# Hash attention and a squared-ReLU feed-forward block: the last pair of the last chunk in wide form, gates moved to ScalarE, second-layer sums by quarters

## The chip, the cores and the metric

The kernel runs on one core of a Trainium2 chip. The metric is the device time of one execution in microseconds. The profile is that of one execution on the same kind of core; its times are counted from its first instruction. The engines are TensorE (PE; PEld is its weight load), VectorE (DVE), ScalarE (ACT), GpSimd (POOL) and SyncE (SP). A "q" behind an engine's name marks its sequencer, which issues DMAs.

## The reference

Attention over hash buckets, and then a feed-forward block on its output:

```python
q_bucket, k_bucket = ...            # six sign bits of q @ proj and of k @ proj
scores = np.where(q_bucket == k_bucket, scale * q @ k.T, -1e9)
attn = softmax(scores);  x = (attn @ v) as (3072, 512)
h = x @ w_in                        # (3072, 2048)
r = np.maximum(h, 0.0);  g = r * r
out = g @ w_out                     # (3072, 512)
```

All values are fp32. The shapes are 4 batches, 8 heads, 768 tokens and 64 dimensions for the attention, and 3072 tokens, 512 inputs and 2048 hidden features for the block. The change touches the block alone.

## The kernel before, in words

**Stages.** Attention comes first, two heads at a time; beside it the weights of the block are read, rounded and stored to DRAM in the forms that the block needs (`round_weight`, `keep_weight`, L185 to L210; the pieces of w_out pass through two buffers named `out_piece`, and L210 stores them). Then come three chunks of 1024 tokens (`i` = 0, 1, 2). Each chunk has a first layer (hidden = x w_in and its gate, the squared ReLU) and a second layer (`project`, out = hidden w_out).

**Products with fewer multiplications.** A product of two 2x2 block matrices is made with seven block products in place of eight (Winograd's form of Strassen's method). The price is sums and differences of blocks before and after. `product` (L972) is the order of these seven: it holds three PSUM accumulators (acc0, acc1, acc2, two buffers each), and `keep` copies partial sums from them to SBUF tiles `one`, `two`, `five` and `three` on ScalarE. Block product 0 opens acc0; 1 goes to acc1; 4, 5 and 2 are added to acc0 one after the other, each after the last partial sum was copied; 3 and 6 go to acc2.

**First layer.** A chunk's 1024 tokens and 2048 hidden features are cut in half, so that a unit of 128 features of the upper and 128 of the lower half needs seven products of 128x128 weights with 512 tokens, each over two blocks of inputs. The results are b11, b12, b21 and b22, each of 8 rows of 128x512. Chunk 0 uses this form alone (`hidden`, L1091). Chunks 1 and 2 work in pairs of units (`n` = 0 to 3, each of two halves) and apply the method a second time inside some of the seven products. A product so treated is seven matmuls of 256 columns for both halves of the pair, in place of four matmuls of 512 columns. `hidden_pair` (L1410) treats three products (A, B, C) so and keeps four as they are; `hidden_wide` (L1314) treats five (A, B, C, D, E) and keeps two. Before the change pairs 0 to 2 of a chunk are wide and pair 3 is `hidden_pair`, in both chunks (L1750). `inner_steps` (L1210) gives the steps of a treated product: its accumulators are acc banks or two side banks (`last0`, `last1`), its intermediate copies go by ScalarE (L1237, L1248, L1251, L1255, L1264) and its adds by VectorE (`add_in`, L1273). Before the change a copy of one partial sum goes into a spare quarter (`spots`) of the tiles of sums.

**Gates.** A gate is either one VectorE instruction that multiplies max(h, 0) with h (`gated`, L1075), or two ScalarE activations in place, Relu and Square (`gate_in`, L1275).

**Order around a pair.** The program's order is the order of each engine's queue; it is written out by hand. `hidden_wide` leaves the end of its work (gates, differences for the second layer) in lists; `behind(m)` runs list m of the pair before at a chosen place of the pair that follows. `hidden_pair` calls `behind` too and leaves nothing. After the first half of pair 3, five `leaf` tiles (w_out parts) are loaded by DMAs that ScalarE issues (`load_leaf`, L1493). `mark` (L1040) squares a piece of q and k on ScalarE with an accumulated maximum, to guard the attention's range; it does not depend on the block.

**Second layer.** `project` (L1568) makes seven products `k` = 0 to 6, each again of seven leaves. `OUTER` (L1475) names the operand of each: b11, b12, b_t, b22, b21, b11, b_t. VectorE makes the sums of these operands as it goes: `inner_sums(k)` makes the two tiles t1, t2 of product k, and the `hook` after its second leaf subtracts t2 from one quarter. Behind product 0 b11 becomes b22 - b_t, and behind product 2 b_t becomes b21 - b11, in two instructions of 2048 elements a partition each (L1693, L1699).

**Memory.** Tiles come from pools that are opened on memory that earlier pools gave back; a tile that lies where an earlier tile was waits for the last users of that one. Pool `p_r` (L953) opens after attention with `one`, NH = 5 tiles `h` (L962, L1083), `two`, `five` and `three`, of 2048 bytes a partition each, in this order, from byte 98,976 on; it lies where the weight stage had its last pieces. `p_k` and `p_y` follow it.

Of the kernel before, what the change touches and what calls it, by code (L numbers as in the profile page):

```python
# [34 lines left out]
def kernel(  # L35
# [686 lines left out]
    def load_unit(n, pool=p_i):  # L722

        if n < NCHUNK * NR and n not in w_unit:
# [13 lines left out]
            if n >= 2 * NR:  # L738
                nc.sync.dma_start(out=five_six(w), in_=w_in_49[pair, :, 3 + half])
# [4 lines left out]
    def sum_unit(n):  # L744


        if NR <= n < 2 * NR and n % NR < NR - 2:
# [6 lines left out]
            nc.gpsimd.dma_start(out=w_in_49[pair, :, 3 + half], in_=five_six(w))  # L754
# [15 lines left out]
    with tc.manual_schedule():  # L770
# [191 lines left out]
        HN, QN, NH = NCH // 2, NCH // 4, 5  # L962
# [9 lines left out]
        def product(n, w, at, bt, c11, c12, c21, c22, hook=None, last=False, beside=None, cuts=1):  # L972
# [16 lines left out]
            def keep(of, name):  # L989
                t = p_r.tile([P, 512], FP32, name=name, bufs=KEPT[name])[:, 0:w]  # L990
                nc.scalar.copy(out=t, in_=acc[of])  # L991
                return t
# [121 lines left out]
        w_inner, t_inner, spots, snaps, now, behind_pair = {}, {}, {}, {}, {}, {}  # L1114
# [77 lines left out]
        def sums_inner(i, js):  # L1192

            for j in js:
                y11, y12, y21, y22 = quarters_x(i, j)
                if j < 3:
                    tile = p_y.tile([P, NQ, QN], FP32, name=f"t{j}", **({"bufs": 2} if j < 2 else {}))
                    t = [tile[:, m] for m in range(NQ - 1)] + [y12]
                    spots[i, j] = tile[:, NQ - 1]
                else:  # L1200
# [3 lines left out]
                t_inner[i, j] = t  # L1204
# [5 lines left out]
        def inner_steps(i, j, side, w):  # L1210

            t1, t2, t4, t3 = t_inner[i, j]
            y11, _, y21, y22 = quarters_x(i, j)
            if i not in snaps:
                snaps[i] = [side_bank(m)[:, 0:QN] for m in range(2)]
            one = three = spots[i, side]
            hs = {}
# [7 lines left out]
            def mul(out, a, b, start, stop):  # L1227
                nc.tensor.matmul(  # L1228
                    out=out, lhsT=w(a), rhs=b, start=start, stop=stop, skip_group_check=True
                )  # L1230

            def step_0():
                a0, a1 = (
                    ps_m.tile([P, 512], FP32, name=f"acc{m}")[:, 0:QN] for m in (0 if j == 4 else 1, 2)
                )
# [5 lines left out]
                hs["a0"] = a0  # L1241

            def step_1():
                last = hs["last"] = (
                    ps_m.tile([P, 512], FP32, name="acc2")[:, 0:QN] if j == 4 else snaps[i][side]
                )
                mul(hs["a0"], 4, t2, False, False)
                nc.scalar.copy(out=hs[0][:, QN:HN], in_=hs["a0"])  # L1248
                mul(last, 3, t1, True, False)
                hs[1] = new(1)  # L1250
                nc.scalar.copy(out=hs[1][:, QN:HN], in_=last)  # L1251

            def step_2():
                mul(hs["a0"], 5, t3, False, False)
                nc.scalar.copy(out=three, in_=hs["a0"])  # L1255
                mul(hs["last"], 6, y22, False, True)

            def adds():
                for unit, by in (0, hs["last"]), (1, three):
                    add_in(hs[unit][:, QN:HN], by)  # L1260

            def step_3():
                mul(hs["a0"], 2, t4, False, True)
                nc.scalar.copy(out=hs[1][:, 0:QN], in_=hs["a0"])  # L1264

            def put(unit, out, other):
                add_in(hs[unit], other)
                gated(out, hs[unit])

            return step_0, step_1, step_2, step_3, put, adds, hs  # L1270
# [43 lines left out]
        def hidden_wide(i, n, half):  # L1314

            r0, r = n, NQ + n
            w, acc, add, keep = outer_steps(i, n, half)
            own = own_factors(w, half)
            if half == 0:
                load_inner(i, n + 1)  # L1320
                load_third_inner(i, n + 1, nc.sync)
                now["A"] = inner_steps(i, 0, 0, w_inner[i, n][0])
                if n == 0:
                    sums_inner(i, (3,))
                now["D"] = inner_steps(i, 3, 1, lambda a: own[a])
            A, D = now["A"], now["D"]
            u0 = D[6]
            add(acc, 0, "11", True, False)
            one = keep(acc, "one")
            if half == 0:  # L1330
# [5 lines left out]
                behind(0)  # L1336
            else:
                B, C = inner_steps(i, 2, 0, w_inner[i, n][2]), inner_steps(i, 1, 1, w_inner[i, n][1])
                E = inner_steps(i, 4, 2, lambda a: own[a])
                B[0]()  # L1340
                C[0]()
                E[0]()
                A[4](1, b11[:, r], one)
                behind(2)
                sum_unit(i * NR + 2 * n + 2)
            add(acc, 4, "t2", False, True)
            two = keep(acc, "two")
            if half == 0:
                A[1]()
                D[1]()  # L1350
                A[2]()
                D[2]()
                A[3]()
                D[3]()
                if n == 0:
                    mark()
                A[5]()
                D[5]()
                add_in(u0[0], two)
                A[4](0, b11[:, r0], one)  # L1360
                sum_unit(i * NR + 2 * n + 1)
                behind(1)
                now["two"] = two
                return
            two_0 = now["two"]
            B[1]()
            C[1]()
            add_in(u0[1], two)
            B[2]()
            C[2]()  # L1370
            B[5]()
            E[1]()
            C[5]()
            B[3]()
            E[2]()
            B[4](0, b12[:, r0], u0[0])
            C[3]()
            E[3]()
            E[5]()
            B[4](1, b12[:, r], u0[1])  # L1380
            hC, hE = C[6], E[6]
            add_to(b22[:, r0], u0[0], hE[0])
            add_to(b22[:, r], u0[1], hE[1])
            add_in(two_0, hE[0])
            add_to(b21[:, r0], hC[0], two_0)
            behind(3)

            def step_0():
                gate_in(b22[:, r0])
                add_in(two, hE[1])  # L1390
                add_to(b21[:, r], hC[1], two)
                for m in r0, r:
                    minus(b_t[:, m], b12[:, m], b11[:, m])
                inner_sums(0, slice(n, n + 1))
                minus(b12[:, r0], b22[:, r0], b12[:, r0])

            def step_1():
                gate_in(b22[:, r])

            def step_2():  # L1400
                gate_in(b21[:, r0])
                minus(b12[:, r], b22[:, r], b12[:, r])

            def step_3():
                gate_in(b21[:, r])

            for m, step in enumerate((step_0, step_1, step_2, step_3)):
                behind_pair[m].append(step)

        def hidden_pair(i, n, half):  # L1410
# [3 lines left out]
            if half == 0:  # L1414
                now["A"], now["C"], now["B"] = (
                    inner_steps(i, j, (0, 0, 1)[j], w_inner[i, n][j]) for j in range(3)
                )
# [6 lines left out]
            else:  # L1424
                B[2]()
                B[5]()
                C[0]()
                A[4](1, b11[:, r], one)
                B[4](0, b12[:, r0], now["two"])
                behind(3)  # L1430
# [14 lines left out]
            if half == 0:  # L1445
                A[2]()
                A[5]()
                B[0]()
                A[4](0, b11[:, r], one)
                add_in(two, five)  # L1450
            else:
                C[2]()
                C[5]()
                add_in(two, five)
                B[4](1, b12[:, r], two)
                minus(b_t[:, r], b12[:, r], b11[:, r])
                inner_sums(0, slice(n, n + 1))
                C[4](0, b21[:, r0], now["three"])
# [8 lines left out]
            else:  # L1467
# [3 lines left out]
                C[4](1, b21[:, r], three)  # L1471
# [95 lines left out]

        def project(i):  # L1568
# [60 lines left out]
            for k in range(7):  # L1629
# [23 lines left out]

                def hook():
                    y21 = b[:, NQ:NR, 0:QN]
                    minus(y21, y21, t2)
                    if marks(i, k):
# [20 lines left out]
                use = uses[k]  # L1678
                product(
                    NQ, QN, a_with_load, bt, lambda *p: use(0, *p), lambda *p: use(1, *p),  # L1680
                    lambda p: use(2, p, None), lambda *p: use(3, *p), hook,
                    (i, k) == (NCHUNK - 1, 6), mark if marks(i, k) else None,
                )
# [302 lines left out]
```

## Time and profile before

| what | value |
|---|---|
| time, median of 3 runs | 850.16 us (849.66 to 850.66) |
| profiled execution: its own time | 851.49 us |
| its span, first to last instruction | 849.9 us |
| granted TensorE clock, mean | 0.999 |
| first layer of chunk 0 starts | 314.06 us |
| first layer of chunk 1 | 494.98 to 584.77 us |
| first layer of chunk 2 | 669.66 to 758.46 us |
| last second layer starts | 758.46 us |

A line of a timeline has the start, the duration, the engine, the line of the kernel, the operation, the tile written and the tiles read, their shapes and the number of instructions merged; square brackets hold the idle time of the engine before it and what ended it. A matmul in fp32 has two records, of half its time each; the duration of a record is longer than the distance to the next because matmuls overlap, so distances of starts are the measure of TensorE's pace. A line of a group has the busy time, the mean of one in ns, and the idle time before them. A line of a stretch has the busy time and count of each engine, the granted clock, the share of the DMA engines and GB/s.

### The profile page before, as it was taken

What the parts mean: (1) busy time and instruction counts of PE and PEld (TensorE: products, weight loads), DVE (VectorE), ACT (ScalarE), POOL (GpSimd) and SP (SyncE); (2) the same over time, 40 slices, a digit from 0 to 9 for tenths busy, and PEclk for the clock granted to TensorE, in tenths of its full rate; (3) what the DMA queues carried; (4) which work ended last, traced back from release to release, by engine and by line L of the source; (5) the groups of instructions that cost most, each with busy time, mean ns of one, the idle gap of its engine ahead of it and who ended that gap; (6) DMA issues with size and microseconds to landing.
All of it is one profiled execution on the core that took longest, in us unless ns stands there. A gap on an engine that the chain in (4) does not pass through costs nothing.

```text
span 849.9 us, 17478 instructions
## 1 busy us (share of the span) xinstructions
PE 841.6 (99%) x6698; PEld 555.4 (65%) x6698; DVE 758.5 (89%) x1087; ACT 439.8 (52%) x833; POOL 171.0 (20%) x289
## 2 busy tenths in 40 slices
PE   9999999999999999999999999999999999999997
PEld 4444444444475445544788877767888777768885
DVE  4898999999999988989899989988988988888876
ACT  5887777878777762222211146775232457753210
POOL 1321121303221201643121220001211300021103
PEclk9999999999999999999999999999999999999999
DMA  9966999989996426999977994418878964157666
GB/s 185 201 130 138 185 186 201 207 173 224 249 245 202 158 69 245 330 312 306 359 254 220 275 226 145 146 50 292 298 214 244 247 207 145 51 169 213 201 166 128
DMA packets 237304, 174.10 MB, mean 205 GB/s; under 512 B 165224, under 2 KB 195248, under 8 KB 237216
## 3 DMA queue, kind: packets, MB, share of 16 engines
q1 hardware_dynamic: 196976, 90.14, 43.3%
q0 software_dynamic: 16992, 44.02, 16.5%
q10 hardware_dynamic: 23248, 38.78, 14.7%
q8 instruction: 54, 0.88, 0.5%
q14 instruction: 34, 0.28, 0.1%
HBM read 129.51 MB, written 42.73 MB: 203 GB/s over the span
## 4 chain that ended last, share of the span: by engine, by line
PE 95%; DMA 2%; DVE 1%; ACTq 0%; issue 0%; ACT 0%; POOL 0%; SPq 0%; POOLq 0%; DVEq 0%
PE acc L984 40%; PE st L478 18%; PE xo L532 14%; PE acc L1228 10%; PE acc L1298 8%; PE last L1228 3%; PE tot L589 1%; PE hash L396 1%; DMA bits<-signed 1%; DMA out_dram<-h 1%; PE tp L342 0%; DMA qk_nat<-in_q_dram 0%; ACTq L1499 0%; DVE h L1522 0%; DVE o L1288 0%
## 5 line engine op out<-in xcount | busy, mean ns | idle before, releaser
L484 ACT ACTIVATE e<-st 128x768 f32<-128x768 f32 x192 | 155.5, 810 | 56.8 <-PE st L478 52.5
L532 PE MATMUL xo<-e,v_nat 64*64 64x385 f32 (+1 forms) x1520 | 156.7, 483 | 0.0
L984 PE MATMUL acc<-b,leaf 128*128 128x256 f32 x600 | 133.1, 379 | 0.0
L984 PEld LDWEIGHTS acc<-b,leaf 128*128 128x128 f32 x600 | 113.9, 190 | 16.1 <-issue 0.5
L478 PE MATMUL st<-feat 64*64 64x384 f32 x1056 | 109.3, 483 | 0.0
L444 POOL DMA_DIRECT2D bits<-signed x120 | 62.1, 522 | 196.5 <-ACT signed L433 194.7
L532 PEld LDWEIGHTS xo<-e,v_nat 64*64 64x64 f32 (+1 forms) x1520 | 58.5, 133 | 65.7 <-issue 54.7
L984 PE MATMUL acc<-t,leaf 128*128 128x256 f32 x336 | 76.1, 379 | 0.0
L984 PEld LDWEIGHTS acc<-t,leaf 128*128 128x128 f32 x336 | 63.7, 190 | 9.1 <-issue 0.3
L478 PE MATMUL st<-bits 64*64 64x384 bf16 x768 | 65.9, 324 | 0.4 <-DMA bits<-signed 0.4
L520 DVE TENSOR_TENSOR total<-total,e 128x1536 f32<-128x1536 f32 x32 | 56.0, 1750 | 7.6 <-ACT e L484 6.9
L1028 POOL DMA_DIRECT2D raw_qk<-in_q_dram x32 | 17.3, 541 | 212.3 <-ACT raw_qk L1033 209.8
L520 DVE TENSOR_TENSOR t_x<-t_x,e 128x1536 f32<-128x1536 f32 x32 | 55.8, 1744 | 3.9 <-ACT e L484 3.8
L478 PEld LDWEIGHTS st<-feat 64*64 64x64 f32 x1056 | 39.8, 133 | 25.6 <-issue 21.7
L984 PE MATMUL acc<-x,w_unit 128*128 128x512 f32 (+1 forms) x144 | 56.5, 546 | 0.0
L984 PE MATMUL acc<-b_t,leaf 128*128 128x256 f32 x240 | 53.8, 379 | 0.0
L991 ACT COPY two<-acc 128x256 f32<-128x256 f32 (+1 forms) x29 | 12.5, 431 | 75.2 <-PE acc L984 59.7
L1076 DVE SCALAR_TENSOR_TENSOR b<-h 128x512 f32<-128x512 f32 x72 | 49.1, 691 | 2.2
L991 ACT COPY one<-acc 128x256 f32<-128x256 f32 (+1 forms) x29 | 12.5, 431 | 72.6 <-PE acc L984 53.3
L984 PEld LDWEIGHTS acc<-b_t,leaf 128*128 128x128 f32 x240 | 45.6, 190 | 6.2
L478 PE MATMUL st<-t_x 64*64 64x384 f32 x480 | 48.9, 482 | 0.0
L478 PEld LDWEIGHTS <-bits 64*64 64x64 bf16 x768 | 24.6, 107 | 35.2 <-issue 32.8
(234 smaller groups left out, 1537.8 us busy)
## 6 DMA issues: line engine op xcount, KB each, us to landing
leaf<-w_out ACTq DMA_DIRECT2D x142, 256.0 KB, 3.4
raw<-in_moe_w_in_dram SPq DMA_DIRECT2D x8, 1024.0 KB, 6.4
raw<-in_moe_w_out_dram SPq DMA_DIRECT2D x8, 1024.0 KB, 7.5
w_unit<-w_in SPq DMA_DIRECT2D x8, 896.0 KB, 8.5
w_out<-sums POOLq DMA_DIRECT2D x16, 448.0 KB, 7.4
v_nat<-in_v_dram SPq DMA_DIRECT2D x16, 384.0 KB, 5.1
x_all<-x_raw SPq DMA_DIRECT2D x16, 384.0 KB, 3.2
raw_qk<-in_q_dram POOLq DMA_DIRECT2D x32, 192.0 KB, 3.6
```

The costliest lines, as they stand in the source:

```text
L396: nc.tensor.matmul(out=banks[g * NR_B:(g + 1) * NR_B, h, 0:HS], lhsT=projs[rows, h * D:h * D + NR_B], rhs=feat[pr][rows, w, c * HS:(c + 1) ...
L444: nc.gpsimd.dma_start(out=t[h * D:h * D + NBITS + 1, w, c * HS:(c + 1) * HS], in_=signed[pr % 2][at:at + NBITS + 1, h],)
L478: nc.tensor.matmul(out=st[k * HK:(k + 1) * HK, h, 0:HS], lhsT=src[1][rows, key], rhs=src[0][rows, cut], start=first, stop=not first, skip_ ...
L484: nc.scalar.activation(out=key_of(pr, kt)[:, :, i, 0:HS], in_=st[:, :, 0:HS], func=ACTF.Exp, scale=scale)
L520: nc.vector.tensor_tensor(out=totals[pr], in0=totals[pr], in1=e, op=ALU.add)
L532: return nc.tensor.matmul(out=outs[pr][h * D:(h + 1) * D, c, 0:HS + 1], lhsT=nat[pr, "v_nat"][rows, h, kt * D:(kt + 1) * D], rhs=key_of(pr ...
L984: nc.tensor.matmul(out=acc[to][:, at_c], lhsT=a(i), rhs=b(i)[:, at_c], start=first and i == 0, stop=last and i == n - 1, skip_group_check= ...
L991: nc.scalar.copy(out=t, in_=acc[of])
L1028: nc.gpsimd.dma_start(out=raw_qk[i][:, w], in_=flat[:, i * n:(i + 1) * n])
L1076: nc.vector.scalar_tensor_tensor(out=out, in0=h, scalar=0.0, in1=h, op0=ALU.max, op1=ALU.mult)
L1228: nc.tensor.matmul(out=out, lhsT=w(a), rhs=b, start=start, stop=stop, skip_group_check=True)
L1298: nc.tensor.matmul(out=to, lhsT=w[:, PLACE[a], f], rhs=bt[b](f), start=first and f == 0, stop=last and f == NFT // 2 - 1, skip_group_check ...
```

## The change

Five things change together.

1. In chunk 2 pair 3 is made by `hidden_wide` too (`i > 1 or ...`). Its own sums of weights are made by VectorE at that time, and not loaded. Its end is not left to the next pair, there being none, but put into the first product of the last second layer: `now["edge"]` holds functions that `project` calls in the hook, and behind its copies of `two`, `five` and `three` (argument `then` of `product`).
2. In `hidden_wide` the gates of b11, and in chunk 1 that of b12's second row, and in the edge pair b12's second row, go from VectorE to ScalarE.
3. In `inner_steps` the first partial sum is copied into h itself and added to there; the spots are gone except for tiles of sums, `last0` and `last1` serve product E alone, and all others use acc1 and acc2. In the first half of a wide pair, A and D come before the outer product; the order of the steps is A, D, outer 0, then A, D steps, outer 4.
4. `hidden_pair` calls `behind(3)` before its step B[2], and `behind(4)` where `behind(3)` was. Lists 0 to 4 of a wide pair are filled with other steps.
5. In `project` the two big differences are made by quarters (`second_sum`, `fourth_sum`): of b11 the upper right behind product 0, the lower left in the hook of product 2, the other two in the hook of product 3; of b_t the upper right behind product 2, the lower left in the hook of product 4, the other two behind product 4.

NH goes from 5 to 6, so pool `p_r` has one more tile of 2048 bytes; tile `t2` is made smaller by 1024 bytes.

```diff
-            if n < NR or pair == NQ - 1:
+            if n < NR or n // NR == 1 and pair == NQ - 1:
...
-        HN, QN, NH = NCH // 2, NCH // 4, 5
+        HN, QN, NH = NCH // 2, NCH // 4, 6
...
             def step_0():
-                mul(a0, 0, y11, True, False)
-                nc.scalar.copy(out=one, in_=a0)
-                mul(a1, 1, y21, True, True)
-                nc.vector.tensor_tensor(out=hs[0][:, 0:QN], in0=a1, in1=one, op=ALU.add)
+                bank(0)
+                bank(1)
+                mul(0, 0, y11, True, False)
+                mul(1, 1, y21, True, True)
+                nc.scalar.copy(out=hs[0][:, 0:QN], in_=banks[0])
+                add_in(hs[0][:, 0:QN], banks[1])
...
             def step_2():
+                mul(0, 5, t_inner[i, j][3], False, False)
+                if direct:
+                    add_in(hs[1][:, QN:HN], banks[0])
+                else:
+                    nc.scalar.copy(out=hs[1][:, 0:QN], in_=banks[0])
+                mul(1, 6, y22, False, True)
+                if not direct:
+                    add_in(hs[1][:, QN:HN], hs[1][:, 0:QN])
+                add_in(hs[0][:, QN:HN], banks[1])
...
+                A[0]()
+                D[0]()
+                if n == 0:
+                    sums_inner(i, (3,))
+                add(acc, 0, "11", True, False)
+                behind(0)
+                one = keep(acc, "one")
+                behind(1)
+                A[1]()
+                D[1]()
+                if n == 0:
+                    mark()
+                A[2]()
+                D[2]()
+                behind(2)
...
+                A[3]()
+                behind(3)
+                D[3]()
+                add_in(D[4][0], two)
+                add_to(b11[:, r0], A[4][0], one)
+                gate_in(b11[:, r0])
...
+            steps = (
+                (sums_0, gates_0), (sums_1,),
+                (sums_2, gates_1, lambda: ahead(both), gates_2),
+                (lambda: inner_sums(0, slice(n, n + 1)), gates_3),
+                (lambda: over(both),),
+            )
...
         def hidden_pair(i, n, half):
             else:
+                behind(3)
                 B[2]()
-                B[5]()
                 C[0]()
-                A[4](1, b11[:, r], one)
-                B[4](0, b12[:, r0], now["two"])
-                behind(3)
+                put(A[4][1], b11[:, r], one)
+                put(B[4][0], b12[:, r0], now["two"])
+                behind(4)
...
+                    if k == 2:
+                        second_sum(*Q21)
+                    if k == 4:
+                        fourth_sum(*Q21)
+                    if k == 3:
+                        second_sum(*Q11)
+                        second_sum(*Q22)
...
                 if k == 0:
-                    for h in range(2):
-                        at_h = slice(h * NQ, (h + 1) * NQ)
-                        minus(b11[:, at_h], b22[:, at_h], b_t[:, at_h])
+                    second_sum(*Q12)
                     inner_sums(2)
                 if k == 2:
-                    for h in range(2):
-                        at_h = slice(h * NQ, (h + 1) * NQ)
-                        minus(b_t[:, at_h], b21[:, at_h], b11[:, at_h])
+                    fourth_sum(*Q12)
                     inner_sums(4)
+                if k == 4:
+                    fourth_sum(*Q11)
+                    fourth_sum(*Q22)
...
-                    (hidden_wide if s // 2 < NQ - 1 else hidden_pair)(i, s // 2, s % 2)
+                    (hidden_wide if i > 1 or s // 2 < NQ - 1 else hidden_pair)(i, s // 2, s % 2)
```

In these lists `gates_0` gates the first row of b22, `gates_1` the second row of b12 (chunk 1 only), `gates_2` the second row of b22 and `gates_3` both rows of b21, each by `gate_in` on ScalarE.

More of the change, by code (lines that the diff above doesn't have):

```diff
@@ L1208, in sums_inner, with inner_steps, bank @@
                 minus(t[3], y22, y12)
-        def inner_steps(i, j, side, w):
-            t1, t2, t4, t3 = t_inner[i, j]
+        def inner_steps(i, j, w):
+            direct = j in (0, 3)
             y11, _, y21, y22 = quarters_x(i, j)
[L1216 to L1219, printed above, removed]
+            hs, banks = {}, {}
+            def bank(m):
+                t = side_bank(m) if j == 4 else ps_m.tile([P, 512], FP32, name=f"acc{m + 1}")
+                banks[m] = t[:, 0:QN]
             def new(unit):
@@ L1321, in hidden_wide @@
                 load_third_inner(i, n + 1, nc.sync)
[L1322 to L1330, printed above, removed]
+                A = now["A"] = inner_steps(i, 0, w_inner[i, n][0])
+                D = now["D"] = inner_steps(i, 3, lambda a: own[a])
                 A[0]()
@@ L1346, in hidden_wide @@
+            E = inner_steps(i, 4, lambda a: own[a])
+            u0 = D[4]
+            add(acc, 0, "11", True, False)
+            one = keep(acc, "one")
+            add_to(b11[:, r], A[4][1], one)
+            B[0]()
+            C[0]()
+            E[0]()
+            gate_in(b11[:, r])
+            behind(4)
+            sum_unit(i * NR + 2 * n + 2)
+            if edge:
+                mark()
             add(acc, 4, "t2", False, True)
             two = keep(acc, "two")
[L1348 to L1364, printed above, removed]
@@ L1452, in hidden_pair @@
                 C[2]()
-                C[5]()
                 add_in(two, five)
-                B[4](1, b12[:, r], two)
+                put(B[4][1], b12[:, r], two)
                 minus(b_t[:, r], b12[:, r], b11[:, r])
                 inner_sums(0, slice(n, n + 1))
-                C[4](0, b21[:, r0], now["three"])
+                put(C[4][0], b21[:, r0], now["three"])
             mark()
```

201 lines of the change are left out of this document (125 added, 76 removed).

## The prediction

> **What bounds the kernel now.** I read the page first, then TensorE's order of time, then windows over the stages that the change touches.
>
> ```profile
> PE 841.6 (99%) x6698; PEld 555.4 (65%) x6698; DVE 758.5 (89%) x1087; ACT 439.8 (52%) x833; POOL 171.0 (20%) x289
> PE 95%; DMA 2%; DVE 1%; ACTq 0%; issue 0%; ACT 0%; POOL 0%; SPq 0%; POOLq 0%; DVEq 0%
> ```
>
> TensorE is busy for the whole span and holds 95% of the chain that ended last. So a microsecond is won only by fewer matmul cycles, and any wait that TensorE meets is paid in full. The windows below are the second layer of the first chunk, then the first layers of the second and the third chunk (columns: stretch, its length, busy time of each engine, granted clock, DMA).
>
> ```profile
> 410.35:494.98 84.63, 84.63 (x394) 74.50 (x392) 80.62 (x128) 11.75 (x31) 18.95 (x30) 1.00 0.87 267
> 494.98:584.77 89.79, 89.61 (x333) 62.77 (x332) 79.03 (x171) 60.29 (x143) 7.94 (x15) 1.00 0.47 149
> 669.66:758.46 88.80, 88.80 (x334) 63.02 (x332) 75.47 (x151) 60.30 (x143) 4.26 (x8) 1.00 0.49 150
> ```
>
> VectorE (third busy figure) has 4 us to spare in the first and 11 to 13 in the others; ScalarE (fourth) has 29. ScalarE has room on average; what counts is what stands in its queue at the moments when TensorE needs a copy.
>
> **The change part by part.** *TensorE's work.* In the built program 8 matmuls with 512 columns go and 14 with 256 come.
>
> ```profile
> 747.20 1.88 PE L1298 MATMUL acc<-x,w_unit 128*128 128x512 f32 x4
> 748.91 0.59 PE L1228 MATMUL acc<-x,leaf 128*128 128x256 f32 x2
> 749.35 0.59 PE L1228 MATMUL last<-x,leaf 128*128 128x256 f32 x2
> ```
>
> Every matmul has two records. By the starts, two of 512 take 1.71 us and one of 256 takes 0.43 to 0.44: 8 x 0.857 - 14 x 0.432 = 0.8 us saved. That is all the arithmetic can bring; every other term is a wait.
>
> *A sixth buffer for h (NH 5 to 6).* It costs no instruction, but it moves addresses. In the built program of before, the first `three` tile lies only on the older of the two `out_piece` buffers of the weight stage; the second one reaches the newer. With six h tiles of 2,048 bytes the first `three` (bytes 119,456 to 121,504) lies on the newer (119,968 to 124,064), and its copy on ScalarE waits for the store of the last weight piece to w_out.
>
> ```profile
> 322.74 7.03 PE L984 MATMUL acc<-x,w_unit 128*128 128x512 f32 x16
> 322.94 0.59 ACT L991 COPY three<-acc 128x512 f32<-128x512 f32 x1 [1.13 <-PE acc L984]
> 326.89 0.33 SPq L210 DMA_DIRECT2D w_out<-out_piece  x1
> DMA to landing us min/median/max: 2.7/3.0/4.7
> ```
>
> The copy ran at 322.94, before that store was even issued. Now it starts at 326.89 + 3.0 = 329.89 and ends at 330.5. TensorE first finishes product 6 (two matmuls, to 322.74 + 1.72 = 324.46); its next one adds to the bank that is being copied. Stall 330.55 - 324.46 = **6.1 us**, 5.8 to 7.8 with the fastest and slowest landing. TensorE has no idle record in this stage that could take it back.
>
> *The clock.* The trace shows what a silent TensorE costs:
>
> ```profile
> 843.85 0.44 PE L1558 MATMUL acc<-ident,o 128*128 128x128 f32 x2 [0.51 <-DVE o L1288]
> 848.00:850.00 2.00, 0.00 (x0) 0.00 (x0) 0.00 (x0) 0.00 (x0) 0.00 (x0) 0.70 0.00 0
> ```
>
> The last matmul ends at 844.3; the granted clock is 1.00 to 848 and 0.70 over the next two microseconds, so if it halves it does so near 848.8, some 4.5 us after the last matmul. A silence of 6.1 us is longer. No row shows a recovery; my estimate is that it takes as long as that silence did, 4.5 us at half rate: **2.2 us** for each stall over 4.5 us, between 0 (no drop) and 3.0 (half rate for 6.1 us). [...]
>
> *Second layer by quarters.* VectorE's elements stay the same, but three quarter sums of 1,024 columns move from behind the third product to the fifth one, and three from behind the first to the third and fourth. At the fourth product VectorE is as late as before; from the fifth on it has 3 x 1.14 + 0.2 = 3.6 us more.
>
> ```profile
> 474.46 1.23 DVE L676 TENSOR_TENSOR b<-b,t 128x1024 f32<-128x1024 f32 x1 [0.75 <-PE acc L984]
> 475.60 0.42 DVE L676 TENSOR_TENSOR t<-x 128x256 f32<-128x256 f32 x1
> 493.80 0.42 DVE L1288 TENSOR_TENSOR tmp<-acc,one 128x256 f32<-128x256 f32 x1
> 494.59 0.42 DVE L1288 TENSOR_TENSOR tmp<-acc,two 128x256 f32<-128x256 f32 x1
> 494.98 1.88 PE L1298 MATMUL acc<-x,w_unit 128*128 128x512 f32 x4
> 497.34 0.71 DVE L1522 STREAM_TRANSPOSE h<-o 128x512 f32<-128x512 f32 x1
> ```
>
> It has one pause there, 0.75, and then none to the end, so it arrives 2.85 us late. The new order starts the second chunk's first pair with A and D on acc1 and acc2 instead of the 512-wide product. On the old time axis: D needs the acc1 read at 493.80, done at 494.22 + 2.85 = 497.07, and could start at 494.98 + 0.86 = 495.84: wait 1.2. Its second matmul needs acc2, free at 497.86: 0.35. After the outer product (1.72) A's next matmul needs acc2, whose add stands behind the closing transpose: 498.05 + 2.85 + 0.42 = 501.3 against 500.45: 0.85. D's next needs its sums, now behind two adds: 0.34 + 0.45 + 0.46 - 0.43 = 0.8. Sum **3.2 us** (0.8, D's sums alone, to 4.5). At the third chunk:
>
> ```profile
> 644.03 0.42 DVE L1288 TENSOR_TENSOR tmp<-acc,two 128x256 f32<-128x256 f32 x1 [0.85 <-PE acc L984]
> 649.14 1.23 DVE L676 TENSOR_TENSOR b<-b,t 128x1024 f32<-128x1024 f32 x1 [1.64 <-PE acc L984]
> 669.66 1.88 PE L1298 MATMUL acc<-x,w_unit 128*128 128x512 f32 x4
> 672.03 0.71 DVE L1522 STREAM_TRANSPOSE h<-o 128x512 f32<-128x512 f32 x1
> ```
>
> The pauses of 0.85 and 1.64 take up 2.5 of the 3.6 us. VectorE is 1.1 late, A's add ends near 674.2 against 673.5, and D's sums follow: 1.5 at most; I take **1.2** (0 to 1.5).
>
> *Gates on ScalarE.* 22 gates leave VectorE; each becomes two ScalarE activations, about 1.2 us by the starts below.
>
> ```profile
> 572.96 1.88 PE L1298 MATMUL acc<-x,w_unit 128*128 128x512 f32 x4
> 573.42 0.63 ACT L1278 ACTIVATE b<-b 128x512 f32<-128x512 f32 x1
> 574.09 0.63 ACT L1081 ACTIVATE b<-b 128x512 f32<-128x512 f32 x1
> 574.17 3.33 ACTq L1499 DMA_DIRECT2D leaf<-w_out  x5
> 576.40 1.88 PE L1298 MATMUL acc<-t_x,w_unit 128*128 128x512 f32 x4
> 578.45 0.70 PE L1228 MATMUL acc<-t,leaf 128*128 128x256 f32 x2 [0.17 <-ACT t L1255]
> 582.52 1.98 PE L1298 MATMUL acc<-t_x,w_unit 128*128 128x512 f32 x4
> 584.34 0.59 PE L1228 MATMUL acc<-t,sum 128*128 128x256 f32 x2
> 748.41 2.26 ACTq L1499 DMA_DIRECT2D leaf<-w_out  x5
> L1309 ACT COPY one<-acc 128x512 f32<-128x512 f32 x8 | 4.7, 585 | 10.1 <-PE acc L1298 7.3 <-DMA leaf<-w_out 2.8
> L1248 ACT COPY h<-acc 128x256 f32<-128x256 f32 x12 | 4.5, 377 | 0.2
> L1033 ACT ACTIVATE raw_qk<-raw_qk 128x768 f32<-128x768 f32 x5 | 4.3, 862 | 0.0
> ```
>
> The worst place is the second chunk's last pair, which stays `hidden_pair`. Its second half now puts behind(3), two whole gates, ahead of B[2], where before one gate's copies stood behind it. ScalarE's queue from 573.4: four activations for b12 and b22 (2.4), five leaf issues (2.8, mean of 3.33 and 2.26, less 0.5 that ran beside an activation), `one` (0.5), four for b21 (2.4), B[2]'s copy (0.4): 581.4. Two VectorE adds (0.9) then free acc2 for the `other` product: 582.3. TensorE is there at 572.96 + 1.72 + 4 x 0.432 = 576.4. Stall **5.8 us** (5.3 to 6.4 by the two issue rows), plus 2.2 for the clock. In its place goes what this pair loses now: 2.05 instead of 1.72 from 576.40 to 578.45, 0.1 from 582.52 to 584.34 and 0.2 right behind these two, **0.6** in all.
>
> ```profile
> 529.87 1.25 PE L1228 MATMUL acc<-t_x,w_unit 128*128 128x256 f32 x4
> 530.96 1.88 PE L1298 MATMUL acc<-t_x,w_unit 128*128 128x512 f32 x4
> w_unit<-w_in SPq DMA_DIRECT2D x5, 384.0 KB, 3.3
> ```
>
> In the third chunk's last pair the same five issues and a gate precede `one`, and TensorE needs that bank after 1.72 + 6 x 0.432 = 4.3 us, or 4.6 with a wait of 0.3 at C[0]. ScalarE has b21's two gates (2.4), a copy (0.3), b11's gate (1.3), the issues (2.26 - 0.5) and `one` (0.5): 6.3. That is 1.7, plus 0.4 for two copies behind two marks in E's last steps: **2.1** (0.5 to 2.8). The other wide pairs wait 0.28 at C[0], because D[3]'s copy stands behind the b21 gates (0.26 + 2.4 + 0.58 = 3.24 against 0.43 + 1.72 + 0.86 = 3.01). In the second chunk two such pairs lose 0.22 already (529.87 to 530.96 is 1.09 for two matmuls that need 0.86), so three times 0.28 plus 0.1: **0.9** (0.2 to 1.5). In the last second layer, `three` of the first product stands behind three gates on ScalarE. VectorE has b12's second row ready 4.9 us after the layer's start (three adds and subtractions of 512 and a gate before it at 0.6 to 0.7, three sums at 0.4, then two of 512); from there ScalarE needs three gates (3.7), a mark (1.0), two copies (0.5) and leaf issues (1.1): 11.2 us against 24 x 0.432 = 10.4: **0.8** (0 to 1.5). The last pair's weight sums are eight VectorE instructions of 128 columns, some 2 us in a stage with 13 to spare, ahead of a b11 add that waits for ScalarE anyway: 0, or 1 if that cover goes. SP issues two loads more there; they land in 3 to 4 us and are asked for two units, some 20 us, ahead: 0.
>
> Sum: -0.8 + 6.1 + 2.2 + 3.2 + 1.2 + 5.8 + 2.2 - 0.6 + 2.1 + 0.9 + 0.8 = **+23.1 us**. The profiled run (span 849.9) took 851.49 and would become 874.6; the median 850.16 becomes **873.2 us**.
>
> **Rivals.** *The clock holds.* For it: the halving was seen once, at the end. Then both 2.2 terms go: 868.8. *The queues give way and only the store wait is left.* Against it: ScalarE's queue is in order and the sums above use its own rows. 850.2 - 0.8 + 6.1 + 2.2 + about 2 = 860. *ScalarE's work fits, and the change is faster.* The price is what TensorE could win: 0.8 and the present waits of the second chunk's pairs (0.6 and twice 0.2): 848.4. It decides at one place first: the last weight store would have to land before 324.46 - 0.65 = 323.8, six microseconds earlier than it does. *Late work piles up.* VectorE's 2.85 us grow by a pause lost elsewhere, and issues go at 3.33 in both places: 880. That the wide form is not built at all is excluded by the 14 matmuls.
>
> **How the numbers follow.** Forecast with one or two clock drops 0.62 (869 to 877), clock holds 0.17, store wait alone 0.07, faster 0.03, pile-up 0.11. The range 863.5 to 878.5 leaves out the faster case, most of the store-alone case and most of the pile-up. A measurement of this kernel tells about 0.2% from no change: faster 0.03, same 0.02, slower 0.95.
>
> **What would show it.** In the profile after: the first `three` copy at about 329.9 with a DMA wait and a TensorE gap near 324.5 to 330.5; granted clock below 1.00 behind it; a second gap of 5 to 6 us in the second chunk's last pair, ended by VectorE, with ScalarE full; four gaps of 0.3 to 1.2 at the start of the second chunk's first layer. No gap at 324 would make the prediction wrong by most of its size.

## The result, and the profile after

The kernel after takes **873.07 us** (median of 6 runs, 871.81 to 873.91) against 850.25 us before (6 runs, 849.66 to 851.5): a ratio of 1.0266 (95% interval 1.0253 to 1.0279), 22.8 us slower. The forecast was 873.2 us. The profiled execution took 873.91 us, its span is 872.4 us.

The page of the kernel after, busy times and the shares of the chain that ended last:

```profile
PE 848.1 (97%) x6710; PEld 558.7 (64%) x6710; DVE 749.0 (86%) x1081; ACT 458.7 (53%) x868; POOL 171.0 (20%) x289
PE 85%; DVE 8%; ACT 3%; DMA 2%; issue 1%; SPq 0%; POOL 0%; DVEq 0%; ACTq 0%; POOLq 0%
```

TensorE has 6.5 us more busy time although its work is 0.8 us less: at a granted clock of 0.50 four records of 512 columns take 3.57 us (593.49 to 597.06) against 1.71 at 1.00 (584.61 to 586.32), which makes 3.6 of it (1.8 us twice, below). The other 3.7 us are not broken down here; the ends of matmuls are modelled in the profile, so that a part of a wait counts as busy (the first is 6.0 us as idle time and 6.2 by the starts). Its share of the chain fell from 95% to 85%; VectorE and ScalarE took that. So the time went into waits of TensorE. Three stretches of the kernel after, the counterparts of those shown of before (second layer of chunk 0, first layer of chunk 1, first layer of chunk 2):

```profile
418.45:503.46 85.01, 84.86 (x393) 74.40 (x392) 78.59 (x126) 11.76 (x31) 18.77 (x30) 1.00 0.83 259
503.46:603.19 99.73, 92.43 (x333) 63.05 (x332) 75.62 (x162) 67.56 (x154) 8.10 (x16) 0.97 0.45 138
687.80:780.67 92.87, 89.95 (x346) 64.57 (x345) 69.06 (x146) 66.75 (x157) 4.82 (x10) 1.00 0.47 146
```

They are 0.4, 9.9 and 4.1 us longer than before; with the first layer of chunk 0 (314.10 to 418.45 against 314.06 to 410.35, 8.1 us) that is the whole difference. The clock column is below 1.00 in the first layer of chunk 1. All of TensorE's longer waits (columns: total, times, longest, in us):

```profile
PE acc L985 <- ACT three L992: 6.0, 1, 6.0
PE acc L1308 <- DVE h L1283: 5.3, 1, 5.3
PE acc L1308 <- ACT one L1319: 1.7, 1, 1.7
```

**Chunk 0.** TensorE, ScalarE and SyncE's queue around the first stall, and two stretches behind it:

```profile
323.22 1.45 PE L985 MATMUL acc<-x,w_unit 128*128 128x512 f32 x3
330.68 5.90 PE L985 MATMUL acc<-x,w_unit 128*128 128x512 f32 x9 [6.01 <-ACT three L992]
...
330.04 0.58 ACT L992 COPY three<-acc 128x512 f32<-128x512 f32 x1 [8.18 <-DMA w_out<-out_piece]
...
326.94 0.33 SPq L210 DMA_DIRECT2D w_out<-out_piece  x1
...
324.60:330.60 6.00, 0.07 (x1) 0.00 (x0) 4.86 (x6) 0.56 (x1) 0.00 (x0) 0.74 0.48 160
330.60:334.20 3.60, 3.52 (x4) 1.51 (x5) 1.39 (x2) 0.02 (x1) 0.00 (x0) 0.50 0.98 326
334.20:336.00 1.80, 1.80 (x6) 0.79 (x5) 0.91 (x2) 0.58 (x1) 0.00 (x0) 0.98 0.99 370
```

The copy to the first `three` waits 8.18 us for the weight store issued at 326.94, and starts at 330.04 (forecast 329.89). TensorE's next start was due at 323.22 + 3 x 0.43 = 324.51 and comes at 330.68: 6.2 us. Then the clock is 0.50 to 334.27 (0.98 over 1.80 us is half rate for 0.07): 3.6 us of work at half rate, 1.8 us lost.

**Start of chunk 1**, TensorE in order of time:

```profile
503.46 1.03 PE L1240 MATMUL acc<-x,sum 128*128 128x256 f32 x4
505.13 1.49 PE L1240 MATMUL acc<-t_x,w_unit 128*128 128x256 f32 x4 [0.64 <-DVE tmp L1298]
506.46 1.88 PE L1308 MATMUL acc<-x,w_unit 128*128 128x512 f32 x4
508.17 0.59 PE L1240 MATMUL acc<-t,sum 128*128 128x256 f32 x2
509.28 0.70 PE L1240 MATMUL acc<-t,sum 128*128 128x256 f32 x2 [0.51 <-DVE h L1283]
510.49 1.10 PE L1240 MATMUL acc<-o,w_unit 128*128 128x256 f32 x4 [0.51 <-ACT h L1259]
511.43 0.81 PE L1240 MATMUL acc<-x,sum 128*128 128x256 f32 x3
```

Four records of 256 columns need 0.86 us (544.14 to 545.00), two 0.43. From start to start the surplus is 0.8, 0.5, 0.0, 0.7, 0.8 and 0.1; with 0.3 just before 503.46 it is 3.2 us. The idle times in brackets are shorter than these distances (0.64 against 0.8, 0.51 against 0.7, 0.51 against 0.8), because the end of a matmul is modelled.

**Last pair of chunk 1**, ScalarE and its queue of DMAs, one add of VectorE, then TensorE and the stretch behind its wait:

```profile
586.92 0.64 ACT L1084 ACTIVATE b<-b 128x512 f32<-128x512 f32 x1
587.00 2.38 ACTq L1561 DMA_DIRECT2D leaf<-w_out  x5
589.43 0.58 ACT L1319 COPY one<-acc 128x512 f32<-128x512 f32 x1 [1.87 <-DMA leaf<-w_out]
...
592.29 0.35 ACT L1266 COPY h<-acc 128x256 f32<-128x256 f32 x1
...
592.67 0.43 DVE L1283 TENSOR_TENSOR h<-h 128x256 f32<-128x256 f32 x1 [2.59 <-ACT h L1266]
...
587.19 1.03 PE L1240 MATMUL acc<-x,sum 128*128 128x256 f32 x4
593.49 3.77 PE L1308 MATMUL acc<-t_x,w_unit 128*128 128x512 f32 x4 [5.27 <-DVE h L1283]
...
593.40:597.00 3.60, 3.51 (x4) 1.51 (x5) 3.53 (x7) 0.00 (x0) 0.00 (x0) 0.50 0.00 0
```

The queue stands as forecast: gates, five issues, `one`, two gates (589.91 to 592.38), and only then B[2]'s copy. The releaser named is VectorE's add, but VectorE itself had waited 2.59 us for the copy (592.67). TensorE was due at 588.05: 5.4 us, and again 3.6 us of work at half clock behind it.

### The profile page after: what moved, and what is told of

It is laid out like the page before. It is cut to its first block, busy times and chain, and to the rows that moved or that the text cites. A ratio compares the mean times of both kernels' runs of the same rounds, so it can differ in the third digit from the quotient of the medians.

```text
span 872.4 us, 17526 instructions
## 1 busy us (share of the span) xinstructions
PE 848.1 (97%) x6710; PEld 558.7 (64%) x6710; DVE 749.0 (86%) x1081; ACT 458.7 (53%) x868; POOL 171.0 (20%) x289
## 4 chain that ended last, share of the span: by engine, by line
PE 85%; DVE 8%; ACT 3%; DMA 2%; issue 1%; SPq 0%; POOL 0%; DVEq 0%; ACTq 0%; POOLq 0%
PE acc L985 32%; PE st L478 18%; PE xo L532 14%; PE acc L1240 9%; PE acc L1308 6%; PE last L1240 2%; PE tot L589 1%; DVE t L676 1%; PE hash L396 1%; DVE b L676 1%; ACT b L1084 1%; ACT b L1288 1%; DVE b_t L676 1%; DVE sum L1298 1%; DMA leaf<-w_out 1%
## 5 line engine op out<-in xcount | busy, mean ns | idle before, releaser
L985 PE MATMUL acc<-x,w_unit 128*128 128x512 f32 (+1 forms) x144 | 58.6, 560 | 6.0 <-ACT three L992 6.0
L985 PEld LDWEIGHTS acc<-x,w_unit 128*128 128x128 f32 x144 | 27.9, 195 | 34.1 <-issue 26.0
```

Of the source, the lines that this page charges most:

```text
L985: nc.tensor.matmul(out=acc[to][:, at_c], lhsT=a(i), rhs=b(i)[:, at_c], start=first and i == 0, stop=last and i == n - 1, skip_group_check= ...
```

## The experiments

Times are medians, with the ratio to the kernel before and its 95% interval.

**e1, the address alone, in the kernel before.**

```diff
         HN, QN, NH = NCH // 2, NCH // 4, 5
+        p_r.tile([P, 256], FP32, name="pad", bufs=1)
```

> The kernel before, with one unused tile of 1 KB put ahead of the others in its row pool, and still five h buffers: nothing is computed otherwise, and the first tile named three comes to lie on the place of both out_piece buffers, as in the kernel after. Theory (the place decides, not the count): the first copy to three waits for the last weight store again, TensorE stands still some 6.2 us in chunk 0 and then loses some 1.9 us more at half clock, so 850.3 + 8.0 = 858.3 us. Rival (the stall belongs to the sixth buffer or to the new order of the gates): 850.3 us. Second rival (the wait comes, but the half clock is an accident of the changed kernel): 856.4 us.

858.97 us, 1.0105 (1.0086 to 1.0124). ScalarE, and a stretch of this kernel:

```profile
329.81 0.59 ACT L992 COPY three<-acc 128x512 f32<-128x512 f32 x1 [8.19 <-DMA w_out<-out_piece]
...
330.45:335.80 5.35, 5.35 (x7) 2.26 (x8) 2.27 (x4) 0.59 (x1) 0.00 (x0) 0.50 1.01 346
```

An unused tile of 1 KB brings the whole chunk-0 loss into the kernel before, half clock included. It is a little more than forecast; the half clock here lasts 5.4 us of work, not 3.6.

**e2, five h in the kernel after.**

```diff
-        HN, QN, NH = NCH // 2, NCH // 4, 6
+        HN, QN, NH = NCH // 2, NCH // 4, 5
```

> The kernel after with five h buffers as before, so that the first three lies on the older out_piece alone. Theory: the chunk-0 wait of 6.2 us and its 1.9 us at half clock go and nothing else moves: 873.1 - 8.0 = 865.1 us. Rival (the new order needs the sixth buffer, because more h tiles are alive in a wide pair): the 8.0 us go but waits for h come in the wide pairs of chunks 1 and 2; with one such wait of 0.3 to 0.6 us in each of six halves, 867 to 869 us. Second rival (the store is late for everybody, another tile waits instead): about 873 us.

864.15 us, 1.0163 (1.0143 to 1.0183). ScalarE:

```profile
323.23 0.58 ACT L992 COPY three<-acc 128x512 f32<-128x512 f32 x1 [1.13 <-PE acc L985]
```

The copy waits for TensorE, as it should, and 8.9 us are back, 0.9 more than forecast. No new wait of TensorE appears: the sixth buffer was not needed.

**e7, six h, another order of tiles.** Unused tiles taken first put `one`, `two`, `three` and `five` ahead of h.

```diff
+        for name in "one", "two", "three", "five":
+            for _ in range(KEPT[name]):
+                p_r.tile([P, 512], FP32, name=name, bufs=KEPT[name])
```

> The kernel after, with six h buffers, but the row pool laid out in the order one, two, three, five, h: three lies low, and the fifth and sixth h come to lie on the newer out_piece. The fifth h is first written in the second unit of chunk 0. Theory (whatever tile lies there waits for the last weight store): now VectorE waits some 8 us with the first gate of the second unit; TensorE can go on until it needs that gate's bank again two units later, so it stands still for some 1 to 3 us, and the half clock comes or not with that: 865.1 + 2.2 = 867.3 us (865.8 to 870). Rival (three alone was the trouble): 865.1 us. Second rival (six buffers as such): 873.1 us.

865.59 us, 1.0186 (1.0165 to 1.0207). By the time alone this lies nearer to the first rival; the trace decides. VectorE, ScalarE, TensorE and a stretch:

```profile
329.19 0.69 DVE L1094 TENSOR_TENSOR h<-acc,two 128x512 f32<-128x512 f32 x1 [1.82 <-DMA w_out<-out_piece]
...
329.16 0.59 ACT L1106 COPY h<-acc 128x512 f32<-128x512 f32 x1 [6.46 <-DMA w_out<-out_piece]
...
330.29 5.44 PE L988 MATMUL acc<-t_x,w_unit 128*128 128x256 f32 x20 [1.35 <-ACT one L995]
...
330.30:334.00 3.70, 3.70 (x13) 2.54 (x14) 2.80 (x5) 0.59 (x1) 0.00 (x0) 1.00 1.00 335
```

The wait for the store moved to the h tiles, as the theory says. VectorE had other work until 327.4, so only 1.82 us of it shows there. What reaches TensorE comes by ScalarE, which the expectation left out: its copy into an h waits 6.46 us, the copy to `one` stands behind it, and TensorE, waiting for `one`, stands still for 1.35 us (about 1.5 by the starts). My 2.2 was too much. The clock stays at 1.00. The tiles that lie there decide, not their number.

**e3, gates later in the last pair of chunk 1.**

```diff
-                behind(3)
                 B[2]()
                 C[0]()
+                behind(3)
```

> The kernel after with the hidden gates of behind(3) placed after the steps B[2] and C[0] in the last pair of chunk 1, instead of ahead of them. Theory (ScalarE's queue ends the wait: four gates, five leaf issues, one, then two more gates ahead of C[0]'s copy): the copy of C[0] comes the 2.4 us of those gates and their sums earlier, the wait falls from 5.4 us to about 3.0 us, so 870.7 us if the clock still halves and 868.8 us if 3.0 us is too short for that. Rival (the leaf issues alone set the wait, or VectorE's sums do): the wait stays at 5.4 us and the time at 873.1 us.

869.15 us, 1.0224 (1.0201 to 1.0247). TensorE and two stretches:

```profile
591.55 3.65 PE L1308 MATMUL acc<-t_x,w_unit 128*128 128x512 f32 x4 [2.86 <-DVE h L1283]
...
588.70:591.40 2.70, 0.00 (x0) 0.00 (x0) 1.36 (x4) 1.55 (x4) 0.00 (x0) 1.00 0.88 266
591.60:594.90 3.30, 3.30 (x4) 1.46 (x5) 3.22 (x7) 1.72 (x3) 0.00 (x0) 0.50 0.40 147
```

The wait falls from 5.3 to 2.9 us, as forecast from the queue. The clock still halves: it drops just when TensorE starts again.

**e6, the five leaf loads on SyncE.**

```diff
-                        load_leaf(n, i == 0)
+                        load_leaf(n, True)
```

> The kernel after with the five early leaf loads of each chunk issued on SyncE's queue in every chunk, as chunk 0 has them, instead of ScalarE's. Theory (five issues of 0.5 us are a part of ScalarE's queue that both last pairs wait for): in chunk 1 the wait falls from 5.4 us to 3.0 to 3.5 us, in chunk 2 the 1.8 us wait of the edge pair goes: 873.1 - 2.2 - 1.8 = 869.1 us, and down to 867.3 us if the half clock in chunk 1 shrinks too. Rival (the gates set both waits, the issues lie in ScalarE's idle time): no change, 873.1 us. Second rival: SyncE's queue brings the leaves later, and the first product of a second layer waits for them; then nothing is gained or it gets slower than 873 us.

867.93 us, 1.0194 (1.0168 to 1.022). ScalarE and TensorE in the last pair of chunk 1:

```profile
587.87 0.57 ACT L1319 COPY one<-acc 128x512 f32<-128x512 f32 x1
...
591.91 3.78 PE L1308 MATMUL acc<-t_x,w_unit 128*128 128x512 f32 x4 [3.29 <-DVE h L1283]
```

`one` follows the gate at once, the wait is 2.0 us shorter, and the 1.7 us wait of the edge pair is gone. Gates and issues together make the queue; each takes 2.0 to 2.4 us of the wait. The four runs lie apart: 865.2 and 866.2 us at a mean granted clock of 0.995, 869.7 and 870.1 us at 0.992. So how long the clock is half differs from run to run, and the median tells the gain only to some 2 us.

**e4, whole sums in chunks 0 and 1.**

```diff
                 if k == 0:
-                    second_sum(*Q12)
+                    if more:
+                        for h in UPPER, LOWER:
+                            second_sum(h, slice(0, HN))
+                    else:
+                        second_sum(*Q12)
```

The same for `fourth_sum` behind product 2; the quarters in the hooks of products 2, 3 and 4 and behind product 4 only `if not more`.

> The kernel after, where in chunks 0 and 1 the second layer's sums on b11 and b_t are made in halves after products 0 and 2 again, as before; the last chunk keeps the quarters. Theory (VectorE enters chunk 1 late because the quarters are put into later products, up to the last one that has room for them): the waits at the start of chunk 1 fall from 3.2 us to about 0.4, those of chunk 2 from 1.3 us to about 0.4, together -3.6 us: 869.5 us. Rival (those waits come from the new order of the first layer's own steps, A[0] and D[0] ahead of the outer product): the waits stay, 873.1 us.

869.35 us, 1.0232 (1.0212 to 1.0252): 3.7 us less than the kernel after, 3.6 forecast. TensorE at the start of chunk 1 has one bracket left:

```profile
507.65 1.10 PE L1240 MATMUL acc<-o,w_unit 128*128 128x256 f32 x4 [0.19 <-DVE o L676]
```

**e5, the old form in the last pair of chunk 2.** `hidden_pair`, the loads and the sums of weights there as before. The wide pairs of chunk 2 still overwrite a quarter of t1 and of t3 that the old form reads, so this pair multiplies other numbers; its instructions are those of the old form.

```diff
-                    (hidden_wide if i > 1 or s // 2 < NQ - 1 else hidden_pair)(i, s // 2, s % 2)
+                    (hidden_wide if s // 2 < NQ - 1 else hidden_pair)(i, s // 2, s % 2)
```

> The kernel after with the old form in the last pair of chunk 2 as well, so that the first half of the change's title is undone and the rest stays. The wide form itself has 0.8 us less TensorE work and cost 2.4 us of waits there, plus 0.3 us for C[0]. Theory (what hurts a pair is ScalarE's queue behind a wide pair, whatever the form): the old form in chunk 2 meets the same queue as in chunk 1, but two gates of 0.6 us less, so a wait of some 4.2 us and 1.8 to 3.1 us of half clock: 873.1 + 0.8 - 2.7 + 4.2 + 2.4 = 877.8 us (877 to 879). Rival (the wide form is what costs, and the old form fits as it did before): 873.1 + 0.8 - 2.4 = 871.5 us.

878.32 us, 1.0328 (1.0309 to 1.0346): 5.2 us slower than the kernel after. TensorE's waits have the same entry as before, now twice:

```profile
PE acc L1308 <- DVE h L1283: 9.4, 2, 5.2
```

So the wide form of the last pair was not what cost; the queue that the wide pair ahead of it leaves to ScalarE was.

**e8, four repairs together.** Five h; `behind(3)` later and, ahead of the last pair of chunk 1, `sums_2` and `gates_1` in list 1; leaves on SyncE; whole sums in chunks 0 and 1.

```diff
+            if (i, n) == (1, NQ - 2):
+                steps = (
+                    steps[0], (sums_1, sums_2, gates_1), (lambda: ahead(both), gates_2),
+                    *steps[3:],
+                )
```

> The kernel after with all repairs together: five h buffers; the gates of behind(3) after B[2] and C[0], and in the pair ahead of the last of chunk 1 two sums and a gate one step earlier; the five leaf loads on SyncE; whole sums of the second layer in chunks 0 and 1. The wide last pair of chunk 2 and the quarters there stay. Theory (these four are the whole loss): what is left of the waits is 1.2 us ahead of C[0], 0.5 us in the edge pair, some 0.8 us ahead of the last second layer, and about 1.5 us at the starts of the chunks and in the last pair of chunk 1, against 1.9 us before, and the TensorE work is 0.8 us less: 850.3 - 0.8 + 4.0 - 1.9 = 851.6 us (850.5 to 853.5). Rival (the terms hide behind one another, so that a new wait takes the place of each that goes): 856 us or more. Rival (with its waits mended the wide last pair pays): 849.5 us or less.

852.55 us (12 runs), 1.0026 (1.0015 to 1.0037). The four repairs give back 20.5 of the 22.8 us, and in the block no wait of TensorE is longer than 0.5 us, so no new wait took their place.

**e9, no gates ahead of C[0].** On top of e8:

```diff
                 A[3]()
-                behind(3)
                 D[3]()
+                behind(3)
...
-                gate_in(b11[:, r0])
...
-            gate_in(b11[:, r])
+            gate_in(b11[:, n:NR:NQ])
```

> The kernel with the four repairs, and in the wide pairs the gates of behind(3) after D[3] and both gates on b11 in one pair of instructions after E[0], so that ScalarE makes no gate between the outer copies and the first copies of the second half. Theory (the 0.4 us ahead of C[0] in each of five wide pairs is ScalarE's queue): these five waits go, 852.55 - 2.0 = 850.6 us, as long as the kernel before, with 0.8 us less TensorE work and as much more waiting. Rival (bank and copy set this wait whatever ScalarE does): 852.5 us, or the wait comes back ahead of the next outer step.

850.73 us (11 runs), 1.0007 (0.9998 to 1.0016). TensorE in the second half of a wide pair of chunk 1, in the kernel after and in e9:

```profile
539.42 1.03 PE L1240 MATMUL acc<-x,leaf 128*128 128x256 f32 x4
540.59 1.13 PE L1240 MATMUL acc<-x,sum 128*128 128x256 f32 x4
541.56 1.03 PE L1240 MATMUL last<-t_x,w_unit 128*128 128x256 f32 x4
```

```profile
529.21 1.03 PE L1240 MATMUL acc<-x,leaf 128*128 128x256 f32 x4
530.08 1.03 PE L1240 MATMUL acc<-x,sum 128*128 128x256 f32 x4
530.94 1.03 PE L1240 MATMUL last<-t_x,w_unit 128*128 128x256 f32 x4
```

1.17 and 0.97 us became 0.87 and 0.86: the 0.4 us ahead of C[0] was ScalarE's queue.

**e10, e9 with the old pair in chunk 2**, its tiles and its arithmetic as in chunk 1 (the edit of e5, and the branch for the last chunk's tiles taken out).

> The kernel of e9 with the old form in the last pair of chunk 2 (and chunk 2's tiles as in chunk 1), so that the two differ in what the title of the change names alone. Theory (with the waits mended the wide form is worth its 0.8 us of matmul work, less 0.4 to 0.6 us of small waits in its edge steps and what the old pair waits): no difference that the times can show, within 0.7 us of e9. Rival (the wide form in itself costs waits that no repair removes): this is 1.5 to 2.5 us faster than e9. Rival (the wide form pays in full): this is 0.8 us or more slower.

851.31 us (11 runs), 1.0018 (1.0008 to 1.0028). The first layer of chunk 2 is 89.1 us in e9 (670.33 to 759.42, starts of its first matmul and of the second layer's) and 89.5 in e10 (670.21 to 759.72). Each of the 11 runs is longer than the median of e9, and the medians differ by 0.6 us (0.2 to 1.1 by resampling the two sets of runs). So the difference does show: with the waits mended the wide form is worth about 0.6 us. Whether that is all of the 0.8 us of its matmul work, the interval leaves open.

**e11, e9 with whole sums in chunk 2 too.**

> The kernel of e9 with whole sums of the second layer in the last chunk too. Theory (there the wide last pair leaves VectorE and ScalarE late, and only the quarters keep the second layer from waiting): a wait of 1 to 2 us appears in the last second layer after its first product, 1.6 us longer than e9. Rival (the quarters cost VectorE as much as they save, in the last chunk as in the others): as long as e9 or shorter.

854.17 us (6 runs), 1.0056 (1.0043 to 1.0069): 3.4 us slower than e9, more than the 1.6 forecast. TensorE, VectorE and a stretch:

```profile
783.11 3.61 PE L985 MATMUL acc<-b,leaf 128*128 128x256 f32 x8 [2.10 <-issue]
...
776.06 2.28 DVE L676 TENSOR_TENSOR b<-b,b_t 128x2048 f32<-128x2048 f32 x1
...
781.79 1.22 DVE L676 TENSOR_TENSOR b<-b,t 128x1024 f32<-128x1024 f32 x1
...
783.15:786.35 3.20, 3.20 (x8) 2.57 (x9) 2.14 (x6) 0.00 (x0) 0.00 (x0) 0.50 0.47 173
```

The wait is 2.1 us. The profile names no releaser; by the program's order these matmuls read the quarter that VectorE subtracts from 781.79 to 783.01, behind the whole sums. The clock halves for 3.3 us of work behind the wait, another 1.7. The quarters pay where the edge steps come late, in the last chunk, and cost where they run into the next first layer.

## Why the prediction was right

The total was right, and so were the mechanisms of its large terms; the sizes add up as follows.

- *TensorE's work*, -0.8: the counts are as forecast (6710 records).
- *NH 5 to 6*, 6.1 forecast, 6.2 measured. Shown from both sides by e1 and e2, and moved to another tile by e7.
- *The clock*, twice 2.2: twice 1.8 here. The step's condition was wrong. It said "2.2 us for each stall over 4.5 us"; the kernel after is at half clock 3.0 us after the last matmul in chunk 0 (324.5 to 327.5) and by 590.35, 2.3 us after it, in chunk 1. e3 shows the drop after 2.9 us without matmuls, e11 after 2.1, while 1.35 (e7) and 1.7 (the edge pair) left the clock at full rate. Both stalls (6.2 and 5.4 us) brought the drop all the same, so the sum did not feel it.
- *Quarter sums*, 3.2 and 1.2: 3.2 at chunk 1, and 1.3 at chunk 2 by the same distances of starts. e4 takes 3.7 of the 4.5 away.
- *The last pair of chunk 1*, 5.8: 5.4, because five issues held ScalarE for 1.9 us (587.56 to 589.43), not the 2.3 of the sum (2.8 less 0.5). The 0.6 of old waits there went, as said.
- *The edge pair*, 2.1: 1.8 for `one` and some 0.5 behind it. TensorE and ScalarE there:

```profile
769.20 1.03 PE L1240 MATMUL last<-t_x,w_unit 128*128 128x256 f32 x4
771.90 1.98 PE L1308 MATMUL acc<-t_x,w_unit 128*128 128x512 f32 x4 [1.68 <-ACT one L1319]
...
771.26 0.58 ACT L1319 COPY one<-acc 128x512 f32<-128x512 f32 x1 [1.90 <-DMA leaf<-w_out]
```

- *C[0]*, 0.9: 1.6. It is 0.41 in each of five wide pairs, where 0.28 was put (its own 3.24 against 3.01 gives 0.23), and new for three only; the two pairs of chunk 1 had lost 0.22 before.
- *`three` in the last second layer*, 0.8: nothing. This is the step that failed. It counted leaf issues (1.1 us) as time of ScalarE:

```profile
786.07 0.63 ACT L1084 ACTIVATE b<-b 128x512 f32<-128x512 f32 x1
786.13 0.33 ACTq L1561 DMA_DIRECT2D leaf<-w_out  x1
...
790.54 0.35 ACT L992 COPY three<-acc 128x256 f32<-128x256 f32 x1
```

The five single issues between 780.88 and 789.30 each ran beside an instruction of ScalarE (786.13 inside 786.07 to 786.70); the row of five at 768.74 had held `one` for 1.90 us. `three` was copied by 790.89, about when TensorE needed it (780.67 + 10.4 = 791.1).

The measured terms are -0.8 + 6.2 + 1.8 + 3.2 + 1.3 + 5.4 + 1.8 - 0.6 + 2.3 + 1.6 = 22.2 us, against 22.5 between the spans; the remaining 0.3 was not broken down. The misses are minus 0.8 for `three`, minus 0.8 for the two clock terms and minus 0.4 for the pair, against plus 0.7 for C[0] and plus 0.4 in small ones. They leave 0.9 us of the 23.1: that the median came within 0.2 us of the forecast is luck, as the clock terms alone can differ by more (below). Of the rivals, the one that the clock holds fell with the traces (0.50 in both places), and that the queues give way fell with e3, e5 and e6.

## What to carry to other kernels

A buffer count is an address for every tile that is allocated after it: before adding one, look which earlier tile each later one comes to lie on, and what the last DMA on that one is (an unused tile of 1 KB made TensorE wait 6.0 us in e1). Work that goes from a busy engine to one with room must be counted in the receiving queue, at the instruction that TensorE waits for next, with the DMA issues that stand in the same queue (in the last pair of chunk 1 two gates made up 2.4 us of the wait and five issues 2.0, e3 and e6). And a saving of 0.8 us of matmuls pays only where every wait that the new order makes is removed first: with all of them mended (e9) the kernel is where it was, and the wide last pair by itself is worth about 0.6 us (e10).

## What the runs showed of the hardware

- The half clock (0.50) lasted 6.8 us in chunk 0 and in chunk 1 of the kernel after (327.5 to 334.3, where 0.74 over the 6.00 us to 330.60 is half rate for 3.1, and 590.3 to 597.1), 6.6 to 7.0 us in e1 (from between 329.05 and 329.15 to between 335.8 and 336.0), and 3.2 to 3.6 us in e3 (from between 591.4 and 591.6 to about 595) and in e11 (from between 782.90 and 783.15 to between 786.35 and 786.50). The work that fell into it was 3.6 us twice in the kernel after, 5.4 us in e1, and 3.4 and 3.3 us in e3 and e11, so the loss was 1.7 to 2.7 us.
- From the last matmul to the drop it was 4.5 us at the end of the kernel before (844.3 to 848.8), 3.0 and 2.3 us in the kernel after, 2.9 us in e3 and 2.1 us in e11. What sets this time, and how long the clock then stays at half, was not shown.
- DMA issues cost ScalarE time in one place and not in another: five in a row held it for 1.9 us (587.56 to 589.43), a single one beside an activation (786.13) for nothing.
